# Packed attention and two mixtures of experts on one core: probabilities applied at the Relu, wider pooling matmuls, one ring of h tiles

## The chip, the cores and the metric

The kernel runs on one core of a Trainium2 chip. The metric is the device time of one execution in microseconds; three runs of the kernel before took 586.90, 586.97 and 588.71 us, the median is 586.97. Engines are named PE (TensorE), DVE (VectorE), ACT (ScalarE), POOL (GpSimd) and SP (the queue that issues nearly all DMAs).

## What is computed

Attention in two steps per batch and head (32 packed queries read 576 tokens, then the tokens read the 32 packed values), a dense mixture of four experts, and a soft mixture of eight experts. All in float32.

```python
p_packed = sm_attn(p, k, v)                 # (4, 8, 32, 64)
x = sm_attn(q, p_packed, p_packed)          # -> (2304, 512)
pr = domain_probs / (domain_probs.sum(-1, keepdims=True) + 1e-09)
for e in range(4):
    h = np.maximum(x @ w1[e], 0.0)          # (2304, 1024)
    y += pr[:, e:e + 1] * (h @ w2[e])
logits = y @ phi                            # (2304, 32)
d = softmax over tokens;  c = softmax over the 32 slots
slot_input = d.T @ y                        # (32, 512)
for e in range(8):                          # 4 slots each
    slot_out[e] = np.maximum(slot_input[e] @ m1[e], 0.0) @ m2[e]
out = c @ slot_out
```

## The kernel before

The mixture's output y is never formed. The logits are the sum over experts of probability times h @ (w2 @ phi), so the kernel first folds w2 with phi into `wphi`, and pooling (d.T @ y) is done on h itself: sums `tacc` of d times probability times h per expert, which meet w2 only once, at the end.

**Head** (to 50.62 us). The two head groups of batch 0 run through `attention`, a generator of 17 steps, in turn, with all tiles preloaded: flips of k, score product `sa`, softmax, `et` transposes, value product `pv`, copies into the packed keys `pkn`, flips of q, score product `sb`, softmax on the natural layout, transposes, and two float32r parts of the result (`a2`). One weight chunk of `wphi_steps` (four groups of transposes `w2t`, four copies, 16 products `pw`, a copy `pt`, a transpose `wp`, a copy) is stepped between them, one step per round, from the first round on. `make_g(0)` comes last.

**Loop**. 4 batches of 32 slots; a batch is 4 experts x 2 halves (`ci`, a chunk of 512 columns of w1) x 4 slots of 128 columns. Slot s: `flip_h(s-1)` on DVE, `mm1(s)` (12 matmuls into two PSUM banks, one for each half of the 576 tokens, then Relu by ACT into `ht`), at the first slot of a chunk `make_g` of the next chunk (the first product with w1 folded with the packed values; ACT rounds, DVE subtracts) and `logits` of the chunk before. In batch 0 two further steps of `wphi_steps` per slot. Then what the table `todo` has for the slot: `spread_p`, `weigh` (logits of an expert times its probability, added up in `la`), the softmax steps of the batch before, its `pooling` in three pieces at slots 5, 6, 7 (`POOL_AT`), and the attention of the next batch, from slots 8 and 12 on. The order on each engine is the order of the program; engines wait for each other by semaphores. PSUM: six banks go round in `mm_ps`, some are kept for a while (four by pooling), two hold the logits.

**Pooling**. For each block of 32 tokens, four row groups and four experts one matmul of 32x32 weights `dp` (d times probability, made by DVE at line 589) with 256 columns of the expert's flipped h tile `hn`; sixteen positions of the array are used in turn.

**Tail**. After the last slot: last logits, softmax, pooling of batch 3, then the products with w2, m1 and m2, whose weights stream through slots of 512 KB (`load_chunk`, line 674), and the output. 22 chunks are fetched before that pooling ends, into memory that is free by then; 16 more buffers open when it ends. Each later chunk takes the buffer of a used one.

Of the kernel before, what the change touches and what calls it, by code (L numbers as in the profile page):

```python
# [18 lines left out]
def tile_packed_attention_moe_softmoe(  # L19
# [37 lines left out]
    HT_BUFS = 5  # L57
    POOL_AT = (5, 6, 7)
    ATT_AT = (8, 12)
    FIN_BYTES = 33 * 1024  # L60
# [9 lines left out]
    hx_pool = ctx.enter_context(tc.tile_pool(name="hx", bufs=1))  # L70
# [3 lines left out]
    hn_pool = main.enter_context(tc.tile_pool(name="hn", bufs=NE))  # L74
# [26 lines left out]
    rep = const.tile([128, 128], F32, name="rep")  # L101
    dpn = const.tile([128, NB, NBLK, NE], F32, name="dpn")
    wphi = const.tile([128, NE * NFT, NSL], F32, name="wphi")
    tacc = const.tile([128, NFT, 4, 32], F32, name="tacc")
# [3 lines left out]
    cts = const.tile([128, S], F32, name="cts")  # L108
    m_run = const.tile([128, NB], F32, name="m_run")
# [6 lines left out]
    hn_n = [0]  # L116

    def hn_tile(name):

        hn_n[0] += 1  # L120
        pl = hx_pool if hn_n[0] % (NE + 1) == (5 + NB * NE + 1) % (NE + 1) else hn_pool
        return pl.tile([128, NBLK, NFT, 32], F32, tag="hn", name=name)
# [37 lines left out]
    def load_w1(t=None):  # L160
# [4 lines left out]
        e, hf = divmod(n % NCH, 2)  # L165
# [14 lines left out]
    def norm_probs():  # L180
        n = NB * NBLK
        s = soft.tile([128, S], F32, tag="sw", name="dps", bufs=3)[:, :n]
# [18 lines left out]
    def wphi_steps(n, after):  # L201
        t = w2_t.pop(n)
        for x in range(4):
# [5 lines left out]
            (dve.tensor_copy if x == 3 else act.copy)(t[:, x, :], ps)  # L209
# [13 lines left out]
        pt = soft.tile([128, S], F32, tag="sw", name=f"pt{n}", bufs=3)[:, :128]  # L223
# [19 lines left out]
    def attention(b, g, tmp, late, gp):  # L243
# [69 lines left out]
        let_go(pt)  # L313
        yield
# [25 lines left out]
        qt = [flip("q", hp) for hp in range(2)]  # L340
        late("q")
# [37 lines left out]
    def att_tmp(tag, name):  # L379
        if tag == "a2":  # L380
            return soft.tile([128, S], F32, tag="sw", name=name, bufs=3)
# [55 lines left out]
    def mm1(s):  # L437
        ci, kf = divmod(s, 4)
        b = ci // NCH
        gg = g_t[ci]  # L440
        ht = ht_pool.tile([128, S], F32, tag="ht", name=f"ht{s}")
        fs = slice(128 * kf, 128 * kf + 128)
        for r in range(2):
# [9 lines left out]
            act.activation(out=ht[:, ts], in_=ps[:, :HS], func=AF.Relu)  # L453
# [4 lines left out]
    def flip_h(s):  # L458
        ci, kf = divmod(s, 4)
        b, ch = divmod(ci, NCH)  # L460
        e, hf = divmod(ch, 2)
        if hf == 0 and kf == 0:
            hn_t[b, e] = hn_tile(f"hn{b}_{e}")
        dve.transpose(  # L464
            out=hn_t[b, e][:, :, 4 * hf + kf, :],
# [3 lines left out]
    def logits(ci):  # L469
        b, ch = divmod(ci, NCH)  # L470
        e, hf = divmod(ch, 2)
        if hf == 0:
            lg_t[b, e] = [bank(6 + r, f"lg{b}_{e}_{r}") for r in range(2)]
        for r in range(2):
            for x in range(4):
                pe.matmul(  # L476
                    lg_t[b, e][r][32 * x : 32 * x + 32, :HS],
# [11 lines left out]
    def sw(name):  # L489
        return soft.tile([128, S], F32, tag="sw", name=name, bufs=3)  # L490
# [92 lines left out]
    def pooling(b, pieces):  # L583
# [25 lines left out]
        for e in range(NE):  # L609
            del hn_t[b, e]  # L610
# [467 lines left out]
```

## Time and profile before

| | us |
|---|---|
| median of three runs | 586.97 |
| the profiled execution | 586.25 |
| its span on the core | 584.5 |
| first h product starts (end of the head) | 50.62 |
| last h product ends | 463.99 |
| pooling of the last batch ends | 488.95 |

The profile is that of one execution, and its span is 1.75 us shorter than the time of the execution. A busy share says how much an engine worked in a stretch; whether its work sets the time of the stretch is read from what it waited for, and from who waited for it. The clock that TensorE was granted is given as a share of its full 2.4 GHz. Matmuls in float32 appear as two records each; "x" counts records.

### The profile page before, as it was taken

The page shows a single profiled execution, that of the slowest core. Times are in us where ns is not written, and L with a number is a line of the kernel's source. Part 1 is how long each engine was busy: PE and PEld are TensorE (multiplying, and loading weights), DVE is VectorE, ACT ScalarE, POOL GpSimd, SP SyncE. Part 2 cuts the span into 40 slices and gives each one's busy share as a digit, 9 for nine tenths or more (in the row PEclk, how much of TensorE's full clock was granted, in tenths as well). Part 3 has the DMA queues.
Part 4 walks back from the last instruction along what each step waited for, and adds up shares of the span by engine and source line. Part 5 has one row for each costly group of instructions (what it writes and reads, how often), then busy time and mean ns, then how long its engine had stood idle before and what let it go on. Part 6 is the DMA issues. An engine that isn't in the chain of part 4 may idle for free.

```text
span 584.5 us, 15311 instructions
## 1 busy us (share of the span) xinstructions
PE 488.0 (83%) x6744; PEld 347.2 (59%) x6744; DVE 295.7 (51%) x546; ACT 205.5 (35%) x495; POOL 67.9 (12%) x78
## 2 busy tenths in 40 slices
PE   2475998898998989999898999989999865896763
PEld 2253786676876656677675667767787743222422
DVE  2176444564766266696727668672665533320202
ACT  0224455443553244455314335541345300400202
POOL 2003000010410020232001022300110102100000
PEclk9986999998999999999999999998999977899798
DMA  8952564555242035653303433293473524999997
GB/s 198 361 131 80 195 202 152 173 163 154 73 146 73 4 116 154 175 172 101 118 4 113 137 91 123 96 316 120 177 257 94 178 93 175 420 407 384 385 374 266
DMA packets 65938, 104.49 MB, mean 179 GB/s; under 512 B 5904, under 2 KB 33040, under 8 KB 65872
## 3 DMA queue, kind: packets, MB, share of 16 engines
q1 hardware_dynamic: 65744, 103.36, 52.9%
q8 instruction: 53, 0.87, 0.6%
q0 software_dynamic: 128, 0.15, 0.2%
q14 instruction: 13, 0.11, 0.1%
HBM read 98.78 MB, written 4.72 MB: 177 GB/s over the span
## 4 chain that ended last, share of the span: by engine, by line
PE 64%; DMA 12%; DVE 10%; SPq 5%; ACT 4%; issue 2%; POOL 0%; ACTq 0%; DVEq 0%; POOLq 0%
PE h L449 35%; PE pb L599 9%; DMA ck<-in_moe_w_dram 7%; PE g L418 6%; SPq L674 4%; PE lg L476 4%; DVE g L428 3%; PE sb L262 2%; PE pv L321 2%; PE w2t L206 2%; PE pw L214 1%; ACT g L427 1%; DMA vx<-in_v_dram 1%; DMA k<-in_k_dram 1%; DMA st<-in_moe_w_dram 1%
## 5 line engine op out<-in xcount | busy, mean ns | idle before, releaser
L449 PE MATMUL h<-a,g 128*128 128x288 f32 x1536 | 228.6, 303 | 20.5 <-ACT g L427 8.5
L449 PEld LDWEIGHTS h<-a,g 128*128 128x128 f32 x1536 | 209.1, 190 | 46.1 <-issue 17.4
L453 ACT ACTIVATE ht<-h 128x288 f32<-128x288 f32 x256 | 105.4, 412 | 189.4 <-PE h L449 178.3
L464 DVE STREAM_TRANSPOSE hn<-ht 128x576 f32<-128x576 f32 x128 | 96.8, 760 | 36.4 <-ACT ht L453 36.0
L428 DVE TENSOR_TENSOR g<-g,g 128x512 fp32r<-128x512 f32 x64 | 41.2, 686 | 81.6 <-ACT g L427 81.6
L599 PE MATMUL pb<-hn,dp 32*32 32x256 f32 x2304 | 53.8, 410 | 15.7 <-DVE dp L589 13.5
L599 PEld LDWEIGHTS pb<-hn,dp 32*32 32x32 f32 x2304 | 36.4, 106 | 30.4 <-issue 14.1
L427 ACT CAST g<-g 128x512 fp32r<-128x512 f32 x64 | 34.4, 589 | 20.9 <-PE g L418 20.9
L476 PE MATMUL lg<-ht,wphi 128*32 128x288 f32 x512 | 37.7, 412 | 0.0
L418 PE MATMUL g<-w,pkn 64*32 64x512 f32 x512 | 35.7, 615 | 0.0
L1004 PE MATMUL so<-ck,hm 128*32 128x256 f32 x256 | 25.7, 411 | 11.7 <-DMA ck<-in_moe_w_dram 11.6
L206 PE MATMUL w2t<-ident,st 128*128 128x128 f32 x128 | 19.7, 288 | 18.2 <-DMA st<-in_moe_w_dram 16.4
L476 PEld LDWEIGHTS lg<-ht,wphi 128*32 128x32 f32 x512 | 13.4, 109 | 32.7 <-issue 23.0
L206 PEld LDWEIGHTS w2t<-ident,st 128*128 128x128 f32 x128 | 15.5, 149 | 23.2 <-DMA st<-in_moe_w_dram 16.8
L589 DVE TENSOR_TENSOR dp<-d,dpn 128x768 f32<-128x768 f32 x12 | 11.5, 958 | 29.3 <-PE pb L599 29.2
L1004 PEld LDWEIGHTS so<-ck,hm 128*32 128x32 f32 x256 | 10.1, 115 | 26.6 <-DMA ck<-in_moe_w_dram 20.9
L508 POOL TENSOR_TENSOR la<-la,lw 128x576 f32<-128x576 f32 x8 | 11.4, 1429 | 114.8 <-DVE lw L506 114.8
L494 POOL COPY ps<-dpn 128x576 f32<-128x576 f32 x16 | 12.7, 796 | 89.7 <-DVE d L551 56.4
L1022 DVE TENSOR_TENSOR rr<-sr,rr 32x256 fp32r<-32x256 f32 x4 | 1.7, 422 | 40.4 <-ACT rr L1020 40.3
L958 PE MATMUL hid<-ck,st 128*32 128x512 f32 x128 | 17.8, 595 | 1.1 <-DMA ck<-in_moe_w_dram 0.6
L565 POOL TENSOR_TENSOR lt<-lt,cm 128x576 f32<-128x576 f32 x4 | 4.6, 1157 | 104.2 <-DVE cm L563 104.2
L214 PE MATMUL pw<-st,tacc 128*32 128x128 f32 x256 | 11.8, 278 | 4.3 <-DVE st L209 4.3
(148 smaller groups left out, 414.8 us busy)
## 6 DMA issues: line engine op xcount, KB each, us to landing
ck<-in_moe_w_dram SPq DMA_DIRECT2D x80, 512.0 KB, 8.1
w<-in_moe_w_dram SPq DMA_DIRECT2D x32, 1024.0 KB, 5.0
st<-in_moe_w_dram SPq DMA_DIRECT2D x8, 1024.0 KB, 5.1
k<-in_k_dram SPq DMA_DIRECT2D x16, 288.0 KB, 3.8
out_dram<-ob SPq DMA_DIRECT2D x12, 384.0 KB, 5.7
v<-in_v_dram SPq DMA_DIRECT2D x18, 192.0 KB, 3.7
q<-in_q_dram SPq DMA_DIRECT2D x12, 288.0 KB, 3.1
vx<-in_v_dram SPq DMA_DIRECT2D x6, 192.0 KB, 7.7
```

The costliest lines, as they stand in the source:

```text
L206: pe.transpose(ps[:, 128 * dc : 128 * dc + 128], t[:, x, 128 * dc : 128 * dc + 128], ident)
L418: pe.matmul(ps[g][c : c + 32, :], pkn_t[b][o : o + 64, g, hp, 0, :], t[o : o + 64, 2 * g + hp, :], start=True, stop=True, tile_position=(o ...
L427: act.copy(gg[:, 0, g], ps[g])
L428: dve.tensor_tensor(out=gg[:, 1, g], in0=ps[g], in1=gg[:, 0, g].bitcast(F32), op=ALU.subtract)
L449: pe.matmul(ps[:, :HS], gg[:, l, g, fs], m[:, ts], start=(g == 0 and i == 0), stop=(g == 1 and i == 2),)
L453: act.activation(out=ht[:, ts], in_=ps[:, :HS], func=AF.Relu)
L464: dve.transpose(out=hn_t[b, e][:, :, 4 * hf + kf, :], in_=ht_t[s].rearrange("p (x t) -> p x t", t=32),)
L476: pe.matmul(lg_t[b, e][r][32 * x : 32 * x + 32, :HS], wphi[:, 4 * ch + x, :], ht_t[4 * ci + x][:, HS * r : HS * r + HS], start=(hf == 0), ...
L599: pe.matmul(pb[c][32 * e : 32 * e + 32, : 32 * NFT], dp[o, x, e, :], hn_t[b, e][o, n * i + x].rearrange("p a b -> p (a b)"), start=(i == 0 ...
L674: sp.dma_start(dst, chunks[i])
L958: pe.matmul(hp[i][32 * e : 32 * e + 32, :], st2[:, dc, 4 * s + e, :], cks[e][:, 512 * i : 512 * i + 512], start=(s == 0 and dc == 0), stop ...
L1004: pe.matmul(so[32 * e : 32 * e + 32, :dw], hm[s][:, x + xl, e, :], cks[e][:, dw * xl : dw * xl + dw], start=(s == 0 and x + xl == 0), stop ...
```

## The change

1. **Probabilities at the Relu.** `mm1` multiplies each Relu value by the expert's probability of the token. The even slots and the first half of odd ones: Relu on ACT, then a multiply in place on POOL. The second half of odd slots: one DVE instruction (maximum with 0, times the probability) straight from PSUM. `weigh`, its tiles and the adds go; the logits of all four experts gather in the same two PSUM banks, which are copied to `la` when the batch is done. The spread probabilities (`pe`) are made one expert ahead.
2. **Pooling.** The weights are d itself, so `dp` goes. One matmul takes 512 columns: the same block of two experts. A matmul for even blocks writes 32 partitions and one for odd blocks the next 32; they are added at the end by products with `fold`, which replace the transposes of `tacc`. `tacc` has twice the width per partition. The last batch is pooled in one piece.
3. **One ring of h tiles.** `hr` holds five tiles; a batch takes four in a fixed turn (`place`), and `order` swaps the experts of a pair where the ring wraps. The ring also serves as buffers of the head, for four weight chunks in place of two, and for tail weights: 4 slots during the last batch and 16 after its pooling.
4. **Head and softmax order.** The q flips move ahead of the value product; the probabilities are normalised in the first round; `wphi_steps` starts in round 8, three steps a round, with all copies on ACT; `make_g(0)` is in round 9. The softmax of a batch starts one slot earlier in the next.

```diff
@@ softmaxes, pooling, mm1 (cut)
+            if r and kf % 2:
+                dve.scalar_tensor_tensor(
+                    out=ht[:, ts], in0=ps[:, :HS], scalar=0.0, in1=pr[:, ts],
+                    op0=ALU.max, op1=ALU.mult,
+                )
+            else:
+                act.activation(out=ht[:, ts], in_=ps[:, :HS], func=AF.Relu)
+                pool.tensor_tensor(out=ht[:, ts], in0=ht[:, ts], in1=pr[:, ts], op=ALU.mult)
...
+        act.copy(la[:, :HS], lg[0][:, :HS])
+        dve.tensor_copy(la[:, HS:], lg[1][:, :HS])
...
-                    for e in range(NE):
-                        pe.matmul(
-                            pb[c][32 * e : 32 * e + 32, : 32 * NFT],
-                            dp[o, x, e, :],
-                            hn_t[b, e][o, n * i + x].rearrange("p a b -> p (a b)"),
+                    for pr in range(2):
+                        lo, hi = sorted(place(b, 2 * pr + k) for k in range(2))
+                        for par in range(2):
+                            m = 64 * pr + 32 * par
+                            pe.matmul(
+                                pb[c][m : m + 32, :],
+                                d[o, x + par, :],
+                                hr[o, lo : hi + 1 : hi - lo, x + par, :],
...
-            if wphi_done[0] < 1:
-                next(wgen)
-        make_g(0)
-        norm_probs()
+            if stage == 0:
+                norm_probs()
+            elif stage in (1, 4):
+                next(spread)
+            if stage == 9:
+                make_g(0)
+            if stage >= 8:
+                for _ in range(3):
+                    next(wgen)
+            stage += 1
...
-        pg[b] = pooling(b, 3)
-        for _ in range(3):
-            next(pg[b])
+        pg[b] = pooling(b, 1)
+        next(pg[b])
+        hr_slots([place(b, i) for i in range(NE)])
+        fill_stream()
```

The order on three engines shows what moved. TensorE at the end of the head, before: the first chunk's product with w1 (`g_0`, `g_1`), then h at once.

```order
L418 MATMUL g_0_466<-w_0_149,pkn_201 32x512 x2
L418 MATMUL g_1_467<-w_0_149,pkn_201 32x512 x2
L449 MATMUL h_0_488<-a_00_459,g_465 128x288 x3
L449 MATMUL h_0_488<-a_01_462,g_465 128x288 x3
L449 MATMUL h_1_496<-a_00_459,g_465 128x288 x3
L449 MATMUL h_1_496<-a_01_462,g_465 128x288 x3
```

After: the end of the fourth weight chunk and the whole fifth stand directly ahead of the first h (the first four stand between g and these rows).

```order
L222 MATMUL pw_589<-hr,tacc 32x128 x16
L235 MATMUL wp_609<-ident,pt_607 128x128
L214 MATMUL w2t_0_618<-ident,hr 128x128 x4
L214 MATMUL w2t_1_624<-ident,hr 128x128 x4
L214 MATMUL w2t_2_630<-ident,hr 128x128 x4
L214 MATMUL w2t_3_636<-ident,hr 128x128 x4
L222 MATMUL pw_642<-hr,tacc 32x128 x16
L235 MATMUL wp_661<-ident,pt_659 128x128
L458 MATMUL h_0_665<-a_00_612,g_403 128x288 x3
```

Five chunks now precede the first h instead of one, and TensorE's queue no longer begins with a chunk's transposes.

DVE in the last batch, before: flips of h (L464), the subtraction of g (L428), and the weighing of an expert's logits (L506).

```order
L464 STREAM_TRANSPOSE hn_1_5267<-ht_5425 128x18x32
L428 TENSOR_TENSOR g_5460<-g_0_5461,g_5460 128x512
L428 TENSOR_TENSOR g_5460<-g_1_5462,g_5460 128x512
L464 STREAM_TRANSPOSE hn_2_5485<-ht_5443 128x18x32
L506 TENSOR_TENSOR lw_5504<-lg_1_0_5370,pe_5403 128x288
L506 TENSOR_TENSOR lw_5504<-lg_1_1_5371,pe_5403 128x288
L464 STREAM_TRANSPOSE hn_2_5485<-ht_5487 128x18x32
```

After, at the same place:

```order
L479 STREAM_TRANSPOSE hr<-ht_5267 128x18x32
L436 TENSOR_TENSOR g_5305<-g_0_5306,g_5305 128x512
L436 TENSOR_TENSOR g_5305<-g_1_5307,g_5305 128x512
L479 STREAM_TRANSPOSE hr<-ht_5286 128x18x32
L463 SCALAR_TENSOR_TENSOR ht_5329<-h_1_5339,pe_5180 128x288
L479 STREAM_TRANSPOSE hr<-ht_5329 128x18x32
L479 STREAM_TRANSPOSE hr<-ht_5348 128x18x32
```

The weighing is gone, and a product of an odd slot (L463) stands between two flips.

DVE in the tail, before: the last rows of the softmax, then the three multiplies for pooling (L589) and the sums.

```order
L544 STREAM_TRANSPOSE lt_5876<-lr_5860 128x288
L551 STREAM_TRANSPOSE d_5879<-dt_5870 128x576
L589 TENSOR_TENSOR dp_5885<-d_5879,dpn 128x768
L589 TENSOR_TENSOR dp_5983<-d_5879,dpn 128x768
L589 TENSOR_TENSOR dp_6081<-d_5879,dpn 128x768
L615 SCALAR_TENSOR_TENSOR tacc<-tacc,rsc_5874,pb_5881 128x8x32
```

After, from the last flip on:

```order
L479 STREAM_TRANSPOSE hr<-ht_5457 128x18x32
L524 COPY la_5494<-lg_1_4621 128x288
L533 TENSOR_REDUCE lmx_5501<-lr_5497 128x1
L533 TENSOR_REDUCE lmx_5501<-lr_5498 128x1
L535 TENSOR_TENSOR m_run<-lmx_5501 128x1
L537 TENSOR_TENSOR m_run<-m_run 128x1
L539 TENSOR_SCALAR nm_5506<-m_run 128x1
L553 STREAM_TRANSPOSE lt_5513<-lr_5497 128x288
L553 STREAM_TRANSPOSE lt_5513<-lr_5498 128x288
L560 STREAM_TRANSPOSE d_5516<-la_5494 128x576
L618 SCALAR_TENSOR_TENSOR tacc<-tacc,rsc_5511,pb_5518 128x16x32
```

Nothing stands between the transposed d and pooling any more, and the sums are twice as wide.

## Rows read from the trace of the kernel before

**Rows 1.** Page; busy by stage: us, PE, PEld, DVE, ACT, POOL, clock, DMA, GB/s.

```profile
PE 488.0 (83%) x6744; PEld 347.2 (59%) x6744; DVE 295.7 (51%) x546; ACT 205.5 (35%) x495; POOL 67.9 (12%) x78
...
0.00:50.62 50.62, 21.62 (x322) 14.74 (x322) 21.39 (x46) 11.55 (x29) 7.89 (x17) 0.93 0.76 219
50.62:171.07 120.45, 111.75 (x1244) 86.39 (x1244) 64.24 (x113) 57.37 (x139) 13.76 (x13) 0.96 0.46 145
463.99:488.95 24.96, 16.60 (x597) 10.79 (x596) 8.38 (x16) 1.67 (x6) 0.00 (x0) 0.86 0.24 87
488.95:584.50 95.55, 64.06 (x512) 26.52 (x512) 20.51 (x50) 15.96 (x30) 6.07 (x13) 0.88 1.00 369
```

**Rows 2.** Timeline of PE, head: start, length, line, operation, [idle before, releaser].

```profile
21.40 1.11 PE L206 MATMUL w2t<-ident,st 128*128 128x128 f32 x4 [16.36 <-DMA st<-in_moe_w_dram]
39.29 1.76 PE L262 MATMUL sb<-ux,pkn 32*32 32x288 f32 x32
50.62 3.50 PE L449 MATMUL h<-a,g 128*128 128x288 f32 x12 [8.54 <-ACT g L427]
```

**Rows 3.** Timelines of the DMA queue of SP and of DVE, head.

```profile
16.58 3.87 SPq L151 DMA_DIRECT2D p<-in_p_dram  x4
36.15 1.44 DVE L248 STREAM_TRANSPOSE tx<-qx 128x576 f32<-128x576 f32 x2
```

**Rows 4.** Groups by line, 50.62 to 171.07: busy, mean ns | idle before, releasers.

```profile
L206 PE MATMUL w2t<-ident,st 128*128 128x128 f32 x108 | 16.1, 282 | 0.5 <-ACT ht L453 0.4
L214 PE MATMUL pw<-st,tacc 128*32 128x128 f32 x224 | 10.4, 278 | 3.9 <-DVE st L209 3.9
L227 PE MATMUL wp<-ident,pt 128*128 128x128 f32 x7 | 2.0, 289 | 0.0
```

**Rows 5.** Busy time by stretch: loop's start, first two pooling pieces of the last batch.

```profile
50.62:57.30 6.68, 6.68 (x37) 4.51 (x37) 3.49 (x7) 2.48 (x6) 1.48 (x2) 0.52 0.07 5
472.51:478.30 5.79, 5.79 (x192) 4.18 (x192) 0.00 (x0) 0.00 (x0) 0.00 (x0) 0.62 0.02 6
479.35:483.36 4.01, 4.01 (x192) 2.81 (x192) 0.00 (x0) 0.00 (x0) 0.00 (x0) 1.00 0.01 4
```

**Rows 6.** Waits of PE: us in total, times, longest.

```profile
PE pb L599 <- DVE dp L589: 13.5, 6, 4.5
PE h L449 <- ACT pkn L336: 5.7, 5, 2.0
```

**Rows 7.** Pooling's group by line; weight loads of 512-column products (clock 1.00).

```profile
L599 PE MATMUL pb<-hn,dp 32*32 32x256 f32 x2304 | 53.8, 410 | 15.7 <-DVE dp L589 13.5 <-issue 2.0
...
508.55:519.99 11.44, 11.44 (x102) 3.33 (x102) 6.53 (x15) 0.00 (x0) 0.00 (x0) 1.00 1.03 415
...
509.44 0.13 PEld L958 LDWEIGHTS hid<-ck,st 128*32 128x32 f32 x4 [0.30 <-issue]
509.87 0.13 PEld L958 LDWEIGHTS hid<-ck,st 128*32 128x32 f32 x4 [0.30 <-issue]
```

**Rows 8.** Groups by line, whole span: operations nearest to the new ones.

```profile
L453 ACT ACTIVATE ht<-h 128x288 f32<-128x288 f32 x256 | 105.4, 412 | 189.4 <-PE h L449 178.3 <-issue 10.3 <-DVE cm L573 0.4
L464 DVE STREAM_TRANSPOSE hn<-ht 128x576 f32<-128x576 f32 x128 | 96.8, 760 | 36.4 <-ACT ht L453 36.0
L508 POOL TENSOR_TENSOR la<-la,lw 128x576 f32<-128x576 f32 x8 | 11.4, 1429 | 114.8 <-DVE lw L506 114.8
L615 DVE SCALAR_TENSOR_TENSOR tacc<-tacc,rsc,pb 128x256 f32<-128x256 f32 x12 | 5.0, 478 | 12.8 <-PE pb L599 12.8
```

**Rows 9.** Timelines of PE and DVE, tail, up to pooling's end.

```profile
466.81 1.24 PE L517 MATMUL lr<-la,rep 128*128 128x288 f32 x4 [1.64 <-DVE la L508]
471.50 0.96 DVE L589 TENSOR_TENSOR dp<-d,dpn 128x768 f32<-128x768 f32 x1
472.51 5.79 PE L599 MATMUL pb<-hn,dp 32*32 32x256 f32 x192 [4.47 <-DVE dp L589]
484.42 4.53 PE L599 MATMUL pb<-hn,dp 32*32 32x256 f32 x192 [1.05 <-DVE dp L589]
```

More of the change, by code (lines that the diff above doesn't have):

```diff
@@ L108, in tile_packed_attention_moe_softmoe @@
     cts = const.tile([128, S], F32, name="cts")
+    hr = const.tile([128, RING, NBLK, NFT * 32], F32, name="hr")
+    flat = [hr[:, i].rearrange("p a b -> p (a b)") for i in range(RING)]
     m_run = const.tile([128, NB], F32, name="m_run")
@@ L113, in sm, with place @@
         return small.tile(shape, F32, tag=tag, name=name)
[L116 to L122, printed above, removed]
+    def place(b, i):
+        return (NE * b + i) % RING
+    order = []
+    for b in range(NB):
+        for i in range(0, NE, 2):
+            up = place(b, i) < place(b, i + 1)
+            order += [i, i + 1] if up else [i + 1, i]
     raw = {}
@@ L313, in attention @@
         let_go(pt)
+        qt = [flip("q", hp) for hp in range(2)]
+        late("q")
         yield
@@ L470, in logits @@
         b, ch = divmod(ci, NCH)
-        e, hf = divmod(ch, 2)
-        if hf == 0:
-            lg_t[b, e] = [bank(6 + r, f"lg{b}_{e}_{r}") for r in range(2)]
+        e, hf = order[ci // 2], ci % 2
+        if ch == 0:
+            lg_t[b] = [bank(6 + r, f"lg{b}_{r}") for r in range(2)]
         for r in range(2):
@@ L519, in softmaxes @@
             )
-        yield
         mx = sm("lmx", [128, 2], f"lmx{b}")
@@ L692, in w1_place, with hr_slots, leftover @@
         return w1_pool.tile([128, 2 * CHUNK], F32, tag="w1", name=name)
-    def hx_place(name):
-        return hx_pool.tile([128, 4 * CHUNK], F32, tag="hn", name=name)
+    def hr_slots(ps):
+        for k in range(0, NBLK * NFT * 32 - CHUNK + 1, CHUNK):
+            for p in ps:
+                add_slots(1, lambda name, p=p, k=k: flat[p][:, k : k + CHUNK])
+    left = NBLK * NFT * 32 // CHUNK * CHUNK
+    def leftover(p, n, k=0):
+        return flat[p][:, left + k : left + k + n]
     def g_place(name):
@@ L722, in tile_packed_attention_moe_softmoe @@
         load_w1()
-        load_w2(1, w2s[1])
+        for n in range(1, W2_BUFS):
+            load_w2(n, w2s[n])
         load_p(1)
@@ L738, in tile_packed_attention_moe_softmoe @@
         )
+        pool.tensor_tensor(
+            out=fold.rearrange("p a s -> p (a s)").rearrange("p (a s) -> p a s", a=2),
+            in0=ident.rearrange("p (a b s) -> p a b s", a=2, b=2)[:, :, 0],
+            in1=ident.rearrange("p (a b s) -> p a b s", a=2, b=2)[:, :, 1],
+            op=ALU.add,
+        )
         wp = mm_ps("warm")
@@ L927, in tile_packed_attention_moe_softmoe @@
             )
-        pool.memset(st2, 0.0)
+        for dc in range(NDC):
+            pool.memset(st2[dc], 0.0)
         for s in range(2):
```

218 lines of the change are left out of this document (101 added, 117 removed).

## The prediction

> **What bounds the kernel now.** I read the page's busy times first, then the busy time by stage, then the waits of TensorE, then the timelines of the two ends. TensorE is busy 488.0 of 584.5 us, and the stages show where it is the limit [rows 1]. In the loop over the 128 slots (50.62 to 463.99; the stage of the first batch is shown, 111.75 busy of 120.45 us) it runs without a pause worth naming, so the loop lasts as long as TensorE's own work plus a few short waits. In the head (to 50.62) it is busy for 21.62 us only: there the limit is a chain of loads, softmax steps and copies. Between 463.99 and 488.95 it waits in part, and the DMA engines stand nearly still (share 0.24). From 488.95 the DMA engines are full (share 1.00, 369 GB/s): the rest of the expert weights streams in, and only its bytes count. So work taken off TensorE in the loop counts in full, and so does any shortening before 488.95; work on DVE, ACT or POOL counts only where TensorE comes to wait for it.
>
> The profiled execution took 586.25 us, 1.75 more than its span; the median of the timed runs is 586.97, 0.7 above it. The sum is made on the span.
>
> **Part 1, the head.** Before, four transposes of tail weights stand first in TensorE's queue and hold it until their load lands at 21.40; the last score product runs from 39.29 to 41.05, and the first h product starts at 50.62, after 8.54 us of waiting [rows 2]. Now those transposes stand behind the value product. What then comes last is the q load. The four p issues of the DMA queue wait for the four q transfers, so these landed between 16.58 and 20.45 [rows 3]. The q flips now stand on DVE ahead of the second value product: two pairs of 1.44 us [rows 3], the second after 20.0, so they end near 24, the copies of the packed keys near 25.5, and the score products near 30.5, 10 us earlier than now. But five weight chunks now stand before the first h product instead of one, and ACT's exponentials and casts stand behind their copies. One chunk costs TensorE 4.2 us (28.4 us for 6.75 chunks [rows 4]), and with ACT's copies in series some 4.7. From 30.5: g 1.1, the rest of the first chunk 3.0, four chunks of 4.7, and 2.5 for two exponentials and two casts that hold ACT's copies: 56.0. The loop starts **5.4 us later** (bounds +0.5 at 4.2 us a chunk and no delay by ACT, +10.3 at 5.2 and twice the delay).
>
> **Part 2, the weight chunks in the loop.** 6.75 chunks stand there now: 16.1 + 10.4 + 2.0 us busy and 3.9 us of waiting for a DVE copy [rows 4], together 32.4. Three stay: 12.6 busy, and each now waits some 0.5 us for its small ACT copy, 14.1. **-18.3 us.** TensorE also entered the loop at a granted clock of 0.52 for 6.68 us [rows 5], near the lower of its levels (1.2 of 2.4 GHz), after its 8.54 us pause. It now comes out of back-to-back chunks, so I take the clock to be full: **-3.2 us** (0.48 of 6.68; zero if it isn't).
>
> **Part 3, pooling in the loop.** The multiply of d by the probabilities goes. TensorE waited 13.5 us for it in all, 6.6 of that in the tail (4.47 and twice 1.05), so **-6.9 us** in the loop [rows 6, 9]; what is late next is d, which is now ready in slot 3 of the batch, while pooling still starts in slot 5. Then the matmuls: 576 records of 256 columns per batch become 288 of 512. The line took 53.8 us [rows 7], of which the last batch took 5.79 + 4.01 + 4.53 = 14.3 [rows 5, 9], so nine pieces share 39.5 us, 4.4 each. What do 96 records of 512 columns take? From below: on four column tiles, weight loads of four 512-column records follow each other every 0.43 us at full clock [rows 7]. If sixteen tiles stream side by side as four do, 96 records are six such groups, 2.6 us. The present pieces run at 192 records in 4.01 us [rows 5], so sixteen take 0.334 us, where half of 0.43 would be 0.215: they are held by something per record (20.9 ns), not by columns. From above: if the cost goes with columns after all, a piece keeps its 4.0 us. I take 2.75 (six groups and a little to fill), the row of the same column count being the nearest: **-14.7 us** (bounds -16 and -3.5).
>
> The Trainium skill speaks against this. TensorE: Matmul & The Clock Gate, section "Back-to-back issue gap", lists 262 cycles for 256 columns and 518 for 512, so halving the count and doubling the width would save a hundredth only. By that rule of the Trainium skill this part would come to -3.5 instead of -14.7. The trace disagrees at 256 columns, where sixteen records take 0.334 us against the 0.215 that their columns need; no row shows sixteen tiles at 512.
>
> **Part 4, Relu and the probabilities.** ACT loses 64 of 256 Relus of 412 ns, DVE gains 64 products from PSUM (nearest row 478 ns for 256 columns), POOL gains 192 multiplies of 128x288 (nearest: 1429 ns for 128x576 with two full operands, so 0.72 each) [rows 8]. Taken out are weighing on DVE and POOL and the pooling multiply, so DVE's sum stays about level and POOL rises by some 127 us to near 195, half of the loop. These hide behind TensorE as long as it never waits for them. New waits: each flip of a slot now waits for POOL (0.72 later), and in odd slots the second half of h leaves its PSUM bank by DVE, behind that flip (0.76 [rows 8]). Without attention the bank comes round three slots later, about 5 us, so 1.5 us are hidden. With banks held by attention or pooling the cover falls to one or two slots. Against it, ACT, whose queue held TensorE 5.7 us at the key copies [rows 6], has less to do. I take **+2 us**, bounds -6 (that wait goes) and +13 (0.2 us at each of 64 odd slots).
>
> **Part 5, the tail.** From the last h (463.99) to the end of pooling (488.95) there are 24.96 us [rows 1]. The log-sum product started at 466.81 [rows 9], 2.82 after; the weighing, for whose last add it waited 1.64, is replaced by a copy of half a tile on each of ACT and DVE, but the logits now wait for the last DVE product, so 2.45. Pooling began 5.70 after that; without the multiply (0.96 [rows 9]) 4.7. The single piece of 288 records is 18 groups of 0.43, 7.7, plus 1.8 because its start falls on a low clock (5.79 against 4.01, at 0.62 and 1.00 [rows 5]): 9.5. In all 16.65: **-8.3 us** (bounds -9.5 and -4). The weight stream starts at its end, as before, but with 21 instead of 22 chunks fetched ahead: 0.524 MB at 369 GB/s, **+1.4 us**. The wider sums into tacc, the sixteen small products that replace eight transposes, and the order of DVE there are free: TensorE waits for DVE's softmax chain meanwhile, and the stream covers that; uncovered the sums alone would cost 1.9 (four of 478 ns [rows 8], twice as wide).
>
> **Sum.** +5.4 - 18.3 - 3.2 - 6.9 - 14.7 + 2 - 8.3 + 1.4 = -42.6; span 541.9, execution 543.7, and 0.7 more for the median: about **545 us**.
>
> **Rivals.** (a) Pooling goes with columns: nine pieces lose 11.2 of the gain and the tail 4.3, **560 us**. For it speaks that the one row at 512 columns is bound by its columns and has four tiles, not sixteen; against it that sixteen records of 256 take 0.334 us and not 0.215. (b) A mild convoy: 0.2 us of waiting at each odd slot for a bank, or the head holding the chunks as badly as the loop did (first h at 67), **557 us**. The attention slots, where DVE already runs late behind packed-key copies, speak for it; DVE's busy share of half speaks against. (c) Slower than before: the chain ACT, POOL, flip, DVE product takes so long that TensorE stands at every odd slot. The gain is eaten at 42.6/64 = 0.67 us per odd slot; the whole chain of 0.72 + 0.76 uncovered costs 95 us, **about 640**, and half of it 593. It needs cover to be nearly absent everywhere, against six banks in the last batch; but if POOL's multiply took 1.9 us rather than 0.72, its 192 of them (365 us) and its other work would alone fill the loop's present 413 us. (d) Better: waits of TensorE for ACT in attention vanish and the first h comes at 52, **534 us**.
>
> **How the numbers follow.** Forecast 0.62, (a) 0.17, (b) 0.10, (c) 0.05, (d) 0.06. The range takes in (a), (b) and most of (d) with the bounds of the head and of new waits: 531 to 566. Faster or slower means by more than 0.3%, about what a measurement of this kernel can tell from no change: faster 0.94, within 0.01, slower 0.05, which is (c).
>
> **What would show it.** In the profile after: first h near 56 and at clock 1.00; five chunks ahead of it on TensorE; no wait of pooling in the loop; 96 records of 512 columns in about 2.75 us (4.0 would be (a)); no new DVE entry of more than a few us among TensorE's waits (many of them: (b) or (c)); POOL's multiply near 0.72 us; 17 us between the last h and the end of pooling, and 97 us from there to the end. Wrong would be above all the head, if ACT's in-order queue delays the softmax further, or a POOL multiply of twice its price.

## The result and the profile after

The changed kernel took **536.71 us** (median of four runs, 533.36 to 538.16), the kernel before 586.93 us beside it: ratio 0.9142, 95% interval 0.9082 to 0.9203. The forecast was 545.0 with a range of 531 to 566. Measured a second time, as changed_again, it took 538.31 against 586.54 (0.9186, 0.9162 to 0.9210). The profiled execution took 538.16 us, its span is 536.3, so the span fell by 48.2 us where 42.6 was forecast.

The page's busy line, and the busy time by stage (us, PE, PEld, DVE, ACT, POOL, granted clock, DMA share, GB/s); they answer to [rows 1]:

```profile
PE 480.0 (89%) x5616; PEld 336.4 (63%) x5616; DVE 295.5 (55%) x558; ACT 184.9 (34%) x443; POOL 205.6 (38%) x266
...
0.00:52.09 52.09, 39.27 (x514) 27.29 (x514) 23.84 (x51) 21.74 (x52) 9.66 (x19) 0.97 0.97 313
52.09:424.25 372.16, 357.10 (x4261) 266.62 (x4261) 244.61 (x446) 145.04 (x355) 189.19 (x231) 1.00 0.41 135
424.25:444.90 20.65, 16.20 (x309) 8.01 (x308) 5.83 (x13) 1.66 (x6) 0.59 (x1) 0.83 0.71 257
...
444.90:536.30 91.40, 67.44 (x537) 34.52 (x536) 21.26 (x50) 16.45 (x30) 6.19 (x16) 0.81 0.97 357
```

TensorE's own work fell by only 8 us (488.0 to 480.0). The other 40 us are idle time that is gone. In the loop its work fell by 28.6 us (385.7 to 357.1); 17.7 of them went into the head (21.62 to 39.27 busy), where it had stood still before. By stage, against the kernel before: head +1.5 (50.62 to 52.09), loop -41.2 (413.37 to 372.16), last h product to end of pooling -4.3 (24.96 to 20.65), from there to the end -4.15 (95.55 to 91.40). TensorE is busy for 357.10 of the loop's 372.16 us, at full clock.

The same groups by line in the loop (52 to 425, PE; busy us, mean ns, idle before and its releasers) and the new operations, from the groups of the whole span:

```profile
L458 PE MATMUL h<-a,g 128*128 128x288 f32 x1536 | 225.9, 301 | 11.1 <-ACT pkn L346 5.7 <-ACT et L319 2.9 <-DVE tacc L618 1.3
...
L604 PE MATMUL pb<-hr,d 32*32 32x512 f32 x864 | 30.6, 598 | 0.0
...
L214 PE MATMUL w2t<-ident,hr 128*128 128x128 f32 x48 | 6.3, 274 | 0.0
...
L222 PE MATMUL pw<-hr,tacc 128*32 128x128 f32 x96 | 3.2, 275 | 0.0
...
L469 POOL TENSOR_TENSOR ht<-ht,pe 128x288 f32<-128x288 f32 x192 | 153.1, 808 | 182.1 <-ACT ht L468 182.0
...
L463 DVE SCALAR_TENSOR_TENSOR ht<-h,pe 128x288 f32<-128x288 f32 x64 | 28.0, 437 | 18.2 <-PE h L458 18.0
```

No row of TensorE's waits in the loop names the POOL multiply (L469) or the DVE product (L463), and pooling has no wait there: what is left is 5.7 us for the key copies, as in [rows 6], smaller waits of attention, and 1.9 us that are new, for pooling's sums on DVE (`tacc`).

The head on TensorE, which answers to [rows 2] (start, length, engine, line, operation, [idle before, releaser]); each row with `w2t` begins one of four weight chunks:

```profile
19.79 3.06 PE L331 MATMUL pv<-hr 96*64 96x32 f32 x96
...
24.23 1.95 PE L270 MATMUL sb<-hr,pkn 32*32 32x288 f32 x64
...
32.32 2.55 PE L214 MATMUL w2t<-ident,hr 128*128 128x128 f32 x16
...
37.29 1.91 PE L214 MATMUL w2t<-ident,hr 128*128 128x128 f32 x16
...
42.54 1.91 PE L214 MATMUL w2t<-ident,hr 128*128 128x128 f32 x16
...
46.92 1.91 PE L214 MATMUL w2t<-ident,hr 128*128 128x128 f32 x16
...
52.09 1.83 PE L458 MATMUL h<-a,g 128*128 128x288 f32 x12
```

Twelve records of h now take 1.83 us at the loop's start, where they took 3.50 [rows 2]: the clock is full.

The tail on TensorE and on the DMA queue of SP, same columns:

```profile
424.25 1.81 PE L491 MATMUL lg<-ht,wphi 128*32 128x288 f32 x16
426.06 1.30 PE L528 MATMUL lr<-la,rep 128*128 128x288 f32 x4
430.83 11.21 PE L604 MATMUL pb<-hr,d 32*32 32x512 f32 x253 [3.47 <-DVE d L560]
443.01 1.90 PE L604 MATMUL pb<-hr,d 32*32 32x512 f32 x35 [0.97 <-issue]
447.14 7.06 PE L917 MATMUL tt<-fold,tacc 128*128 128x64 f32 x32 [2.22 <-DVE den L564]
...
434.92 14.06 SPq L677 DMA_DIRECT2D hr<-in_moe_w_dram  x16
457.41 4.23 SPq L677 DMA_DIRECT2D ck<-in_moe_w_dram  x9
```

The load at 434.92 is the one to look at: the weight stream starts ten microseconds before pooling ends (444.90). The forecast had it start at pooling's end.

### The profile page after: what moved, and what is told of

The parts are those of the page before. It is cut to its first block, busy times and chain, and to the rows that moved or that the text cites. A ratio compares the mean times of both kernels' runs of the same rounds, so it can differ in the third digit from the quotient of the medians.

```text
span 536.3 us, 13273 instructions
## 1 busy us (share of the span) xinstructions
PE 480.0 (89%) x5616; PEld 336.4 (63%) x5616; DVE 295.5 (55%) x558; ACT 184.9 (34%) x443; POOL 205.6 (38%) x266
## 4 chain that ended last, share of the span: by engine, by line
PE 76%; DVE 7%; ACT 6%; DMA 4%; SPq 4%; issue 2%; DVEq 0%; ACTq 0%
PE h L458 37%; PE pb L604 8%; PE g L426 6%; PE lg L491 5%; SPq L677 3%; PE hid L982 3%; DVE g L436 3%; PE pv L331 2%; PE w2t L214 2%; PE pw L222 2%; DMA ck<-in_moe_w_dram 2%; PE si L930 2%; PE sb L270 2%; ACT hr L217 2%; PE o L1063 1%
## 5 line engine op out<-in xcount | busy, mean ns | idle before, releaser
L458 PE MATMUL h<-a,g 128*128 128x288 f32 x1536 | 225.9, 301 | 11.1 <-ACT pkn L346 5.7
L469 POOL TENSOR_TENSOR ht<-ht,pe 128x288 f32<-128x288 f32 x192 | 153.1, 808 | 182.1 <-ACT ht L468 182.0
L468 ACT ACTIVATE ht<-h 128x288 f32<-128x288 f32 x192 | 79.1, 412 | 188.4 <-PE h L458 177.5
L479 DVE STREAM_TRANSPOSE hr<-ht 128x576 f32<-128x576 f32 x128 | 97.8, 764 | 47.5 <-POOL ht L469 44.4
L436 DVE TENSOR_TENSOR g<-g,g 128x512 fp32r<-128x512 f32 x64 | 41.2, 685 | 54.4 <-ACT g L435 54.0
L604 PE MATMUL pb<-hr,d 32*32 32x512 f32 x1152 | 43.8, 635 | 4.4 <-DVE d L560 3.5
L463 DVE SCALAR_TENSOR_TENSOR ht<-h,pe 128x288 f32<-128x288 f32 x64 | 28.0, 437 | 18.2 <-PE h L458 18.0
L604 PEld LDWEIGHTS pb<-hr,d 32*32 32x32 f32 x1152 | 19.5, 106 | 21.6 <-issue 13.6
L217 ACT COPY hr<-w2t 128x512 f32<-128x512 f32 x32 | 16.9, 595 | 4.7 <-PE w2t L214 4.6
L1028 PE MATMUL so<-hr,hm 128*32 128x256 f32 x144 | 15.1, 410 | 3.7 <-DMA hr<-in_moe_w_dram 3.7
L214 PE MATMUL w2t<-ident,hr 128*128 128x128 f32 x128 | 16.8, 281 | 1.4 <-DVE g L436 1.4
L214 PEld LDWEIGHTS w2t<-ident,hr 128*128 128x128 f32 x128 | 14.9, 145 | 3.7 <-DVE g L436 2.3
```

Of the source, the lines that this page charges most:

```text
L214: pe.transpose(ps[:, 128 * dc : 128 * dc + 128], t[:, x, 128 * dc : 128 * dc + 128], ident)
L436: dve.tensor_tensor(out=gg[:, 1, g], in0=ps[g], in1=gg[:, 0, g].bitcast(F32), op=ALU.subtract)
L458: pe.matmul(ps[:, :HS], gg[:, l, g, fs], m[:, ts], start=(g == 0 and i == 0), stop=(g == 1 and i == 2),)
L463: dve.scalar_tensor_tensor(out=ht[:, ts], in0=ps[:, :HS], scalar=0.0, in1=pr[:, ts], op0=ALU.max, op1=ALU.mult,)
L469: pool.tensor_tensor(out=ht[:, ts], in0=ht[:, ts], in1=pr[:, ts], op=ALU.mult)
L479: dve.transpose(out=hr[:, place(b, i), :, f0 : f0 + 32], in_=ht_t[s].rearrange("p (x t) -> p x t", t=32),)
```

## Experiments

Twelve runs. The changed kernel itself took 536.71, 538.31 and, with one edit that moved nothing (rows_inner), 537.6 us; differences below are taken against that, or inside the profiles.

**Pooling: what a matmul of 512 columns costs.** The forecast took 96 records of 512 columns to last 2.75 us; they last 3.40. Four runs asked why, the fourth after a stop that the third showed.

split256:

```diff
-   pe.matmul(pb[c][m : m + 32, :], d[o, x + par, :], hr[o, lo : hi + 1 : hi - lo, x + par, :], ...)
+   for j, pl in enumerate((lo, hi)):
+       pe.matmul(pb[c][m : m + 32, 256 * j : 256 * j + 256], d[o, x + par, :], hr[o, pl, x + par, :], ...)
```

> The changed kernel with each pooling product of 512 columns issued as two of 256, one for each expert; nothing else moves. Theory (a record has a fixed cost of about 0.12 us per sixteen records, and its columns add to it): sixteen records of 256 columns take 0.334 us as in the kernel before, so a loop piece goes from 3.35 to 4.0 us; nine pieces add 5.9 us and the single piece of the tail 1 to 2.5: about 544 us. Rival (columns alone set the pace, the kernel before was slow at 256 columns because of something else that is gone): no change, 537. Rival (a record costs the same at either width, which is what the forecast assumed): pieces go to about 6.7, 30 us more, 567.

Measured 581.45 us (ratio 0.9911, 0.9873 to 0.9949). No theory had this: twice the records took nearly twice the time (6.51 against 3.40 us a piece), although each had half the columns. Yet the kernel before had run 192 records of 256 columns in 4.01 us [rows 5]. What differed was the order: here a tile of the array is used twice in a row.

rows_inner (the four row groups next to each other instead of the four column tiles):

```diff
-   for c in range(4):
-       o = slice(32 * c, 32 * c + 32)
-       for pr in range(2):
-           lo, hi = sorted(place(b, 2 * pr + k) for k in range(2))
-           for par in range(2):
+   for pr in range(2):
+       lo, hi = sorted(place(b, 2 * pr + k) for k in range(2))
+       for par in range(2):
+           for c in range(4):
+               o = slice(32 * c, 32 * c + 32)
```

> The changed kernel with the order of the sixteen pooling products of two positions turned: the four row groups follow each other, and the column tile moves slowest; before, the column tiles followed each other on one row group. Theory (the fixed part of a record does not depend on which tile comes next): pieces stay at 3.35 us, 537 us. Rival (the fixed part comes from four products in a row that share a row group and wait for each other's weights or rows): pieces fall to 2.6 to 2.75 us, six groups of 0.43, and the time falls by 6 to 8 us, 530.

Measured 537.6 us (0.9167, 0.9133 to 0.9202), pieces unchanged. As the theory said: which different tile comes next doesn't matter.

split_far (all sixteen tiles with the first half of the columns, then all sixteen with the second):

```diff
+   for j in range(2):
+       for c in range(4):
...
+           for pr in range(2):
+               pl = sorted(place(b, 2 * pr + k) for k in range(2))[j]
+               for par in range(2):
...
+                   pe.matmul(pb[c][m : m + 32, 256 * j : 256 * j + 256], d[o, x + par, :], hr[o, pl, x + par, :], ...)
```

> As split256, two products of 256 columns in place of each of 512, but all sixteen tiles first take the first expert of each pair and then all sixteen the second one, so that a tile comes again only after sixteen records, as in the kernel before. In split256 a record of 256 columns cost as much as one of 512 (34 to 39 ns). Theory 1 (there each tile was taken twice in a row, and that was the cost; away from it a record has a fixed part of about 0.12 us per sixteen plus its columns): sixteen records take 0.334 us again, a loop piece 4.0 us, about 544 us. Theory 2 (a record costs the same at either width in this kernel, whatever the order): pieces of 6.5 us, 581 us.

Timeline of PE: a piece of split256, then split_far (one piece of the loop without a stop, then the tail), and one of the changed kernel:

```profile
163.27 6.51 PE L605 MATMUL pb<-hr,d 32*32 32x256 f32 x192
```

```profile
160.97 4.01 PE L605 MATMUL pb<-hr,d 32*32 32x256 f32 x192
...
439.89 7.20 PE L605 MATMUL pb<-hr,d 32*32 32x256 f32 x285 [3.47 <-DVE d L560]
448.80 3.80 PE L605 MATMUL pb<-hr,d 32*32 32x256 f32 x128 [1.71 <-issue]
455.00 4.51 PE L605 MATMUL pb<-hr,d 32*32 32x256 f32 x128 [2.39 <-issue]
461.46 1.91 PE L605 MATMUL pb<-hr,d 32*32 32x256 f32 x35 [1.96 <-issue]
```

```profile
161.03 3.40 PE L604 MATMUL pb<-hr,d 32*32 32x512 f32 x96
```

Away from itself a tile is as quick as before: 4.01 us. So sixteen records take 0.334 us at 256 columns (4.01 / 12) and 0.567 at 512 (3.40 / 6), the start and end of a piece included. Two lengths of piece at full clock take these ends out: at 256 columns 4.01 us for 192 records and 2.74 for 128 (split_far_late, below) leave 0.318 for sixteen, at 512 columns 9.78 for 288 (warm_softmax, below) and 3.40 for 96 leave 0.532. The difference, 0.214, is the columns' time at the 0.43 us per 512 of [rows 7] (0.215), and what is left at either width is 0.10 us. Theory 1 holds for the pieces, at these two widths: **a fixed part and a part by columns that add**. The tile twice in a row as the cause in split256 follows from the same two runs, which differ in the order of the records alone. The time, 557.44 us, was 13 us off the theory's 544, and the rows show where: between the records stand stops with no releaser ("issue"), 8.9 us in all, in the tail at every 128th record. With its weight load that is every 256th record of TensorE.

The Trainium skill, Runtime: NRT & Kernel Launch, section "Instruction fetch mechanics", says that an engine's instructions are fetched in blocks of 256, ahead of use and mostly hidden. The spacing of the stops agrees; that they are hidden does not hold here, since they cost 6.1 us in one pooling (the packets that show the fetches stand behind the next run).

split_far_late (split_far, and the ring's buffers handed out from the last positions to the first):

```diff
-   for k in range(0, NBLK * NFT * 32 - CHUNK + 1, CHUNK):
+   ks = range(0, NBLK * NFT * 32 - CHUNK + 1, CHUNK)
+   for k in reversed(ks) if back else ks:
        for p in ps:
            add_slots(1, lambda name, p=p, k=k: flat[p][:, k : k + CHUNK])
...
-   hr_slots([place(b, i) for i in range(NE)])
+   hr_slots([place(b, i) for i in range(NE)], back=True)
```

> split_far (557.44 us) with the ring's buffers handed to the stream in reverse order, as in late_slots. In split_far TensorE stood still inside pooling for nothing that the profile names, 8.9 us in all, and in the tail 1.7 to 2.4 us before every 128th record, which with its weight loads is every 256th instruction, while the weight stream ran; the pieces without such a stop took 4.01 us. Theory (TensorE's instructions come late when records are short and the DMA engines are full): without the stream the tail's stops shrink from 6.1 us to under 1.5; pooling there takes 15 to 18 us instead of 23.5, and against it the late stream costs 7 to 8: 556 to 560 us in all. Rival (the stops belong to the count of instructions alone): they stay near 6 us, pooling 23 us, 564 us.

Measured 556.33 us (0.9488, 0.9455 to 0.952). Timeline of PE and of the DMA queue, tail:

```profile
441.00 7.28 PE L605 MATMUL pb<-hr,d 32*32 32x256 f32 x285 [3.47 <-DVE d L560]
448.82 2.74 PE L605 MATMUL pb<-hr,d 32*32 32x256 f32 x128 [0.55 <-issue]
452.28 2.74 PE L605 MATMUL pb<-hr,d 32*32 32x256 f32 x128 [0.71 <-issue]
456.00 1.05 PE L605 MATMUL pb<-hr,d 32*32 32x256 f32 x35 [0.98 <-issue]
...
453.79 14.83 SPq L678 DMA_DIRECT2D hr<-in_moe_w_dram  x16
```

The stream now starts at 453.79; the stops at the same three places shrink from 6.06 to 2.24 us, 128 records fall from 3.80 and 4.51 to 2.74, and pooling takes 16.05 us instead of 23.48. The stream makes the stops longer; a rest of 0.55 to 0.98 us per stop is there without it, 2.24 in all where the theory had under 1.5. The records are longer by the clock. Busy time of the pooling line (PE, PEld, granted clock, DMA share, GB/s), two stretches between stops in split_far, then one in split_far_late:

```profile
448.80:452.60 3.80, 3.80 (x128) 2.53 (x128) 0.65 1.01 391
455.00:459.51 4.51, 4.51 (x128) 2.89 (x128) 0.50 1.03 421
...
448.82:451.56 2.74, 2.74 (x128) 1.83 (x128) 1.00 0.02 6
```

That the stops are instructions arriving late can be seen in the DMA queue q8, "instruction" (packets, MB, share of 16 engines): the changed kernel, split_far, then split_far from 452.50 to 455.00 and split_far_late from 448.82 to 451.57.

```profile
q8 instruction: 44, 0.72, 0.5%
...
q8 instruction: 53, 0.87, 0.6%
...
q8 instruction: 1, 0.02, 2.2%
...
q8 instruction: 1, 0.02, 2.0%
```

The packets are of 16 KB, one for every 256 records of TensorE (11232 in the changed kernel, 13536 in split_far). All seven stops in the last poolings of these three runs end 1.3 to 1.6 us after such a packet is through. Without the stream the next packet starts 1.0 to 1.1 us after a stop, while TensorE works; with it 3.8 to 4.2 us after, and none between 448.80 and 452.50. Why it starts later, no row shows.

**The weight stream.** late_slots (the same reversal in the changed kernel):

> The changed kernel with the ring's buffers handed to the weight stream from the last positions to the first, so that the first load after the loop must wait for nearly all of pooling. Theory (the stream's start sets the end: it starts at 434.92, ten us before pooling ends, because buffers are freed in the order in which pooling goes through the positions, and from there the DMA engines are full): it now starts near 443.5, and the time rises by 6 to 9 us, to about 544. Rival (the early start is worth nothing, because the first products of the tail or the pause of the DMA queue near 449 to 457 set the end): no change, within 1 us of 537.

Measured 544.81 us (0.9285, 0.925 to 0.932), 7.2 more than rows_inner on the same chip; the first load went out at 443.91:

```profile
443.91 15.22 SPq L677 DMA_DIRECT2D hr<-in_moe_w_dram  x16
```

The early start is real, and worth 7 us by the medians. From the start of the log-sum products to the end it is 114.0 us, against 110.2 in the changed kernel's profile and 107.3 in changed_again's, so 3.8 to 6.7: two executions of the same tail differ by 3 us there, with a granted clock of 0.50 and of 0.72 over the last 17 us.

warm_softmax, warm_and_fold_first and warm_all tried to use that; `keep_warm(n)` is n transposes of the identity into a spare bank:

```diff
+   keep_warm(26)
    pg[b] = pooling(b, 1)
```

> The changed kernel with 26 transposes of the identity on TensorE between the last log-sum products and the last pooling, which otherwise follow each other with a pause of 3.5 us, after which the granted clock was 0.50 for some 4 us of pooling. Theory (the pause lowers the clock, the low clock delays the freeing of the first buffers and with it the stream): clock near 1.00 from the start, pooling 10 to 11.5 us instead of 14.07, first load 1.5 to 2 us earlier, time 1.5 to 2.5 us less. Rival (the clock falls for another reason, or the stream has slack there): within 0.5 us of the changed kernel.

```diff
    next(pg[b])
...
+   for e2 in range(2):
+       ps = mm_ps(f"tt{e2}")
...
+       (act.copy if e2 else dve.tensor_copy)(leftover(1 + e2, 512), ps)
    for _ in sg[b]:
        pass
-   for e2 in range(2):
-       ps = mm_ps(f"tt{e2}")
...
+                       if d0 and s and xl == 0 and e < 3:
+                           keep_warm(8, wq)
...
+       if d0:
+           keep_warm(8, wq)
```

> As warm_softmax, and two edits more: the small products that fold the sums and their copies stand ahead of the rest of the column softmax, so that the copies no longer wait 6 us behind it on DVE and ACT; and transposes of the identity fill TensorE's waits for the last chunks and for the last copies. Theory (the end is set by the stream's start and by what follows its last byte, which now runs at a granted clock of 0.50 from 520 on): 1.5 to 2.5 us from the earlier stream, up to 1 from a shorter pause of the DMA queue at 449 to 457, and 2 to 3 at the end: 5 to 6 us less than the changed kernel. Rival (only the stream counts): the same time as warm_softmax.

```diff
    next(pg[b])
+   keep_warm(18, mm_ps("wq"))
```

> warm_and_fold_first with 18 more transposes of the identity between the last pooling and the fold products, which ran at a granted clock of 0.50 and took 7.06 us. Theory (a pause of 2 us ahead of them lowers the clock, and their end sets when the used buffers come free for the stream): fold products in 3.5 to 4 us, the pause of the DMA queue 3 us shorter, and up to 1 us off the end: 533 us, 3 to 4 less than changed_again. Rival (the DMA engines have enough queued over that pause): as warm_and_fold_first, 534 us, 2 to 3 less than changed_again.

> The changed kernel itself, on the same chip and beside the same runs of the kernel before: 535 to 538 us; the measure for the others of this call.

| run | us | ratio to before, 95% |
|---|---|---|
| warm_softmax | 534.51 | 0.9125, 0.9097 to 0.9153 |
| warm_and_fold_first (run beside warm_softmax) | 534.01 | 0.9132, 0.9112 to 0.9152 |
| warm_all | 536.15 | 0.9151, 0.9124 to 0.9178 |
| changed_again (run beside warm_all) | 538.31 | 0.9186, 0.9162 to 0.9210 |

Busy time by stretch of the last pooling (clock after the five engines), then timelines: changed kernel, warm_softmax, warm_all.

```profile
430.83:434.80 3.97, 3.97 (x71) 1.65 (x77) 0.00 (x0) 0.00 (x0) 0.00 (x0) 0.50 0.09 37
434.80:437.80 3.00, 3.00 (x87) 1.89 (x82) 0.00 (x0) 0.00 (x0) 0.00 (x0) 0.73 0.58 187
```

```profile
430.41 9.78 PE L604 MATMUL pb<-hr,d 32*32 32x512 f32 x288 [0.63 <-DVE d L560]
...
432.75 14.44 SPq L677 DMA_DIRECT2D hr<-in_moe_w_dram  x16
```

```profile
444.67 3.76 PE L897 MATMUL tt<-fold,tacc 128*128 128x64 f32 x32
...
435.28 14.22 SPq L677 DMA_DIRECT2D hr<-in_moe_w_dram  x16
450.45 10.55 SPq L677 DMA_DIRECT2D ck<-in_moe_w_dram  x9
```

After its pause of 3.47 us TensorE ran pooling at a granted clock of 0.50, its lower level; filled with transposes the pause leaves pooling at full clock, 9.78 us instead of 14.07, and the first load comes 7.11 us after the start of the log-sum products instead of 8.86 (8.30 in changed_again). The time falls by 2 us or so, by the medians of warm_all and changed_again, whose intervals overlap a little; the changed kernel was not run beside warm_softmax. The further edits did what they were to do inside TensorE (fold products 3.76 us instead of 7.06, the DMA queue's pause of 8.4 us gone) and gave nothing: the three warm runs took 534.0 to 536.2 us. The rival's reading, that the DMA engines had enough queued over that pause, fits. So **what counts here is when the stream starts**, not what TensorE does behind that. From the first load to the end the ten profiles with pooling at 512 columns have 97.5 to 101.7 us, a spread that none of these edits explains.

**The chain ACT, POOL, flip, DVE product.** pool_twice_odd and relu_act_pool:

```diff
    pool.tensor_tensor(out=ht[:, ts], in0=ht[:, ts], in1=pr[:, ts], op=ALU.mult)
+   if kf % 2:
+       pool.tensor_tensor(out=ht[:, ts], in0=ht[:, ts], in1=pr[:, ts], op=ALU.mult)
```

> The changed kernel with POOL's multiply of the first half made twice in the 64 odd slots (the output then carries the probability squared there): 0.81 us more on the chain ACT, POOL, flip, DVE product of just these slots, and 52 us more of POOL in all. Theory (the chain is hidden behind TensorE with room to spare): 537 to 540 us. Rival (the chain was just hidden, each odd slot gives its 0.81 us to TensorE): up to 52 us more, 589.

```diff
-   if r and kf % 2:
-       dve.scalar_tensor_tensor(... op0=ALU.max, op1=ALU.mult)
-   else:
-       act.activation(...); pool.tensor_tensor(...)
+   act.activation(...); pool.tensor_tensor(...)
```

> The changed kernel without the DVE product: all 256 halves of h go through ACT's Relu and POOL's multiply (ACT +26 us, POOL +52 us, DVE -28 us). Theory (the three engines are hidden behind TensorE but for a few places where POOL is behind, as pool_twice_odd showed with the same 52 us on POOL): 3 to 8 us more than the changed kernel. Rival (the DVE product is what frees the banks in time, and without it TensorE waits for ACT at odd slots): 0.4 us at each of 64, 26 us more. Rival (DVE was the late one, at the flips): 1 to 3 us less.

Measured 544.06 us (0.9273, 0.9229 to 0.9316) and 544.64 us (0.9295, 0.9261 to 0.9329). PE's waits in the whole of pool_twice_odd's loop, the rows that are new or lead:

```profile
PE h L458 <- ACT pkn L346: 5.7, 6, 1.0
PE lg L493 <- POOL ht L471: 3.7, 3, 1.2
PE h L458 <- ACT et L319: 2.9, 3, 1.0
```

51 us more on POOL cost 6 to 7, and not at 64 places but at the logits of one chunk in each batch, three of them in the loop with 1.2 us each (the logits' busy time also rose, from 36.5 to 39.6 us). The cover is there at nearly every odd slot, and has a margin of less than 0.8 us at those. Handing the DVE products back to ACT and POOL costs as much, 6.3 us against changed_again: again the logits rise to 39.6, and the waits for ACT's exponentials from 0.7 to 2.9.

**The head.** chunks_in_loop (one weight chunk ahead of the first h product, as before):

```diff
-   if stage >= 8:
+   if stage >= 8 and wphi_done[0] < 1:
        for _ in range(3):
            next(wgen)
```

> The changed kernel with one weight chunk ahead of the first h product, as in the kernel before, and the other seven in the loop; the order of the rest of the head stays new. Theory (the place of the chunks is worth about 6 us, and the rest of what head and chunks gave comes from the earlier score products): first h near 36 instead of 52, four more chunks of 4.7 to 4.8 us in the loop (+19), half clock at the loop's start for some 6.7 us (+3.2): about 543 us. Rival (chunks in the head cost as much as in the loop, the gain is the order of the head alone): within 2 us of 537. Rival (the whole 22 us that head, chunks and clock gave hang on the place of the chunks): 558 us.

Measured 545.78 us (0.9319, 0.9297 to 0.9341), 7.5 to 9 more. Timeline of PE:

```profile
19.95 5.34 PE L331 MATMUL pv<-hr 96*64 96x32 f32 x96
...
43.42 0.61 PE L458 MATMUL h<-a,g 128*128 128x288 f32 x1 [5.96 <-ACT a L382]
```

The first h comes only 8.7 us earlier than in the changed kernel, not 16. The attention's own chain (exponentials, transposes, casts) holds it: TensorE waits 5.96 us for ACT's cast. And the value product of this execution took 5.34 us, not 3.06, though nothing ahead of it was changed: the granted clock was 0.50 from 17 to 26 us, and the score products ended at 30.6 instead of 26.2. 3.25 chunks went over to the loop (100 transpose records there instead of 48, sixteen to a chunk), 14 to 17 us of TensorE's time at 4.4 to 5.3 each, of which the head had taken 8.7. In the loop, with its start at half clock again, they cost 18.3 us (last h at 433.84, worked out as the log-sum products' start less the 1.81 of the logits). 18.3 - 8.7 = 9.6, the 9.5 by which the span is longer. Against changed_again, whose value product took 5.34 us too (first h at 54.26, last at 427.32), the head is 10.8 us shorter and the loop 17.4 longer: 6.5. So the place of the chunks is worth 6.5 to 9.6 us.

## Why the prediction was nearly right, point by point

**Head, +5.4 forecast, +1.5 measured.** The step that failed is "What then comes last is the q load". Issue and landing of the four q loads (us to landing last), and the first q flips:

```profile
8.45 3.61 SPq L138 DMA_DIRECT2D hr<-in_q_dram  x4
...
hr<-in_q_dram SPq DMA_DIRECT2D x4, 288.0 KB, 6.0
...
18.95 1.42 DVE L256 STREAM_TRANSPOSE hr<-hr 128x576 f32<-128x576 f32 x2
```

The loads were issued by 12.1 and took some 6 us, so they were there when the flips began at 18.95, behind other work of DVE and without a wait. (In the kernel before, too, they were issued from 8.6 to 12.2 and landed 6.4 to 7.9 us later, well before 20.45.) The flips ended at 22.0, not 24. What came last were the value product (to 22.85) and the copies of its packed keys (to 24.2); the score products ended at 26.2, not 30.5. Behind them g and the rest of the first chunk took 6.1 us instead of 4.1, and the four chunks with what ACT put between them 19.8 instead of 21.3 (4.4 to 5.3 each). A part is chance: of the twelve profiles with this head, seven have a value product of 3.0 to 3.5 us and the first h at 51.5 to 52.4, five have 5.34 us and 54.0 to 55.0. The profiled execution is one of the seven.

**Chunks -18.3 and clock -3.2: measured -20.6 and -3.3.** Products 28.4 us before, 10.8 after; waits 4.3 before, 1.3 after; the h products fell from 228.6 to 225.9 busy and g by 0.5. Head, chunks and clock together gave 22. chunks_in_loop shows that the place of the chunks is worth 6.5 to 9.6 of it; with one chunk ahead of it either way, the first h came at 43.42 instead of 50.62, so at least 7.2 are the earlier chain (that execution had the value product of 5.34 us); the rest was not taken apart (2.4 of it are half a chunk less in that run's loop, at 4.8 us a chunk).

**Pooling's multiply, -6.9: right.** No wait of pooling is left in the loop. Four stops with no releaser inside its pieces, 2.0 us, are gone as well, which the forecast did not have.

**Pooling's products, -14.7 forecast, -9.0 measured** (39.6 to 30.6). The mis-sized term. The forecast read the 0.334 us for sixteen records of 256 columns as a floor per record that hides the columns, so 512 columns were to cost 0.43. The two add: 0.567, or 0.532 without a piece's ends. Rival (a), and the page's rule that it named (Trainium skill, TensorE: Matmul & The Clock Gate, section "Back-to-back issue gap", twice the columns at twice the time), would have kept a piece at 4.0: 3.40 was measured, about half-way. The bounds held; the choice between them should have been made by what both rows allow together, a sum.

**New waits, +2 forecast, -0.8 measured.** TensorE's other waits in the loop went from 14.5 to 13.7: those for ACT's exponentials fell from 3.1 to 0.7, those for the key copies stayed at 5.7, and the 1.9 for pooling's sums came in, which are twice as wide. POOL's multiply took 0.81 us, not 0.72. The convoy (rivals b and c) did not come; doubling POOL's multiply in the odd slots cost 6 to 7 of the 52 us that a convoy there would have.

**Tail to pooling's end, -8.3 forecast, -4.3 measured.** The steps to its start were right within 0.6 us (log-sum products 1.81 us after the last h, pooling 4.77 later). The single piece took 14.07 us instead of 9.5: nearly 4 of its first us at a clock of 0.50 and 3 more at 0.73, where 1.8 us had been allowed, a stop of 0.97, and the dearer records (12.5 in changed_again). warm_softmax gives 9.78 at full clock and without a stop, where the forecast had 7.7: so 2.1 are the records, and 4.3 the clock and the stop.

**The stream, +1.4 forecast, -4.15 measured.** The step that failed outright: "the weight stream starts at its end, as before". Before, its buffers were opened when pooling was done. In the ring a buffer of 1024 columns is four positions of one tile, pooling goes through the positions in the same order, and a load waits for the last product that reads its own four. late_slots took that away and lost 7 us. The start came 10 us before pooling's end, but the gain is 5.6 against the forecast: from the first load to the end it is 101.4 us, where it was 95.6 before. One load more is 1.4 of that; the rest was not taken apart, but TensorE's granted clock over the last 17 us was 0.50, and 0.85 before.

The sum, +1.5 - 41.2 - 4.3 - 4.2, is the 48.2. Its errors partly cancelled: pooling cost 10 us more than forecast in loop and tail, and head, chunks, waits, stops and stream together gave some 16 more. That the span came within 6 us of the forecast is in part luck. (The terms as written add up to 544.4, not 545.)

## What to carry to other kernels

When buffers are handed to a load queue, look up which instruction really frees each of them: here the order in which slots were listed was worth some 7 us, without any faster engine. When two rows give two possible limits of an operation (per record, per column), try their sum before the larger of them. And keep TensorE fed through a wait like the 3.5 us here, ahead of work that frees something.

## What the runs showed of the hardware

- 32x32 tiles in turn, two records for one float32 product: 0.334 us for sixteen records of 256 columns, 0.567 for 512, with the ends of a piece (0.318 and 0.532 without); in whichever order of different tiles. The same tile twice in a row: 6.51 us for 192 records instead of 4.01.
- TensorE's instructions come in packets of 16 KB, one for 256 records. With records of 21 ns it stops for them: 0.24 to 1.21 us a stop in split_far and split_far_late without the tail's weight stream, 1.71 to 2.39 with it.
- POOL's multiply of 128x288 by a second full operand takes 808 ns, a little more than half of 128x576.
- After a pause of 3.47 us TensorE's granted clock stood at 0.50 over the first 5.6 us of pooling; with 26 small transposes in the pause it was 1.00.
- The same instructions in the head ran with a value product of 3.0 to 3.5 us in seven profiles and of 5.34 in six, for which the clock records have 0.50 in five.
